# Scaling by g on the transposed tile, row products on the general-purpose engine, stores behind the transposes, and a third group of half products in one block

## The chip, the core and the metric

The kernel runs on one core of one Trainium2 chip. The core has five engines that run side by side and wait for each other by semaphores: TensorE (PE: matrix products; its weight loads are shown as PEld), VectorE (DVE), ScalarE (ACT), GpSimd (POOL) and SyncE (SP, which here issues DMAs). Sixteen DMA engines move data. The metric is the device time of one execution in microseconds (us), the median of several runs. The runs of one kernel lay within 0.1 to 0.6% of each other here. All runs used here were in the fast state.

## The reference

```python
kv  = einsum('bhsd,bhse->bhde', k, v)          # linear attention, 8 batches, 8 heads, 576 tokens, 64 wide
o   = einsum('bhsd,bhde->bhse', q, kv)
x   = o / sqrt(mean(o*o, -1) + 1e-6) * g_norm  # then as rows: x is [4608, 512]
g   = x @ w_gate;  val = x @ w_val             # 512 -> 1536
ffn = (gelu(g) * val) @ w_out                  # 1536 -> 512
out = x + sigmoid(x @ w_res) * ffn
```

The factor g_norm belongs to a column of x. In a row tile (tokens on partitions) it is a row vector of 512 values that is multiplied in element by element. In the transposed tile (columns on partitions) it is one scalar for each partition.

## The kernel before

The tokens are cut into nine blocks of 512: blocks 0 to 7 are the first 512 tokens of the eight batches, and the last block holds the remaining 64 of each. For each block there are groups of gate and value products (three groups of four columns of 128, "gps" and "vps" where they are direct), then the "outs": the residual gate and the product with w_out. The attention of a later block is fitted in between.

A group of 2x2 quarters may be done with seven products of half size instead of eight ("half products", Strassen's scheme). It needs sums of weights (wsg, wsv) and of tokens (ts), both made by DVE, and it has inner sums of its own: ACT copies A into E ("seed") and F into d ("keep"), DVE makes F = A + d and c = A + d, and PE then goes on in the same banks. Its order of work is a list of words; other work is hung onto words:

```python
"1g 1v Eg 5g Ev 5v dg 6g dv 6v Fg 2g Fv 2v 7g g11 7v cg 3g cv 3v h11 g12 4g g21 h12 4v g22 h21 h22"
# 1g..7v: products on PE; E, d: copies on ACT; F, c: sums on DVE; g..: gelu on ACT; h..: hid on DVE, h22 on POOL
```

In the kernel before, blocks 3 to 6 are "whole" (all three groups are half products) and block 2 has one direct group in front of two others. Blocks 7 and 8 have three such groups too, but the program does not count them as whole. Shortened, with names simplified and some lines joined:

```python
WHOLE = 3
GROUPS = {2: (1, 2), 3: (0, 1, 2), ..., 6: (0, 1, 2), 7: (1, 0, 2), 8: (0, 1, 2)}

def a_x(b, j, eng=nc.vector):            # g, on the rows, on DVE
    eng.tensor_tensor(out=t[:, j, :], in0=t[:, j, :], in1=g16, op=mult)
...
def first_two():                         # first half of a block's outs
    ...
    nc.scalar.copy(out=w["d"], in_=w["D"])
    aside("gates")
    for j in range(NJ):
        m_sigmoid(j)                     # ACT
...
def others():                            # second half
    prod(w["A"], s_[1], wo_t[:, 1], False);  aside("F")
    sub(nc.vector, w["F"], w["A"], w["d"], ADD);  aside("00")
    prod(w["E"], ...);  pf((0, 0), w["E"]);  aside("22")        # pf: gate product on DVE
    prod(w["A"], ...)
    c22 = res_all[...];  sub(nc.vector, c22, w["A"], w["d"], ADD);  aside("01")
    prod(w["F"], ...);  pf((0, 1), w["F"]);  aside("11")
    prod(w["A"], ...)                    # the last output product, in the bank that c22 was read from
    if whole(blk + 1):
        pf((1, 1), c22, nc.gpsimd);  pf((1, 0), w["A"])         # one gate product on POOL
    else:
        pf((1, 1), c22);  pf((1, 0), w["A"])
    for i in (1, 0):                     # + x on POOL, then the store
        fin((i, i));  fin((i, 1 - i));  store(i)
```

The transposes of x are DMAs issued by SP. In blocks 6 and later the residual gate is done in half products too, interleaved with the four sums hid_s of the hidden tile on DVE.

Of the kernel before, what the change touches and what calls it, by code (L numbers as in the profile page):

```python
# [18 lines left out]
def kernel(  # L19
# [307 lines left out]
    def where(b, j):  # L327
        return (b, j) if j < NJ else (B, pair(b))
# [22 lines left out]
        )  # L351

    def a_x(b, j, eng=nc.vector):
        blk, jj = where(b, j)
        eng.tensor_tensor(out=t_t[blk][:, jj, :], in0=t_t[blk][:, jj, :], in1=g16, op=ALU.mult)  # L355


    def d_qT(b):
# [222 lines left out]
    def res_in_halves(blk):  # L581
        return blk >= LAST[0] - 1

    def out_by_products(blk, later, banks, amid):
        w = {}
        s_ = hid_sums

        def aside(ahead_of):
            for f in amid.get(ahead_of, ()):
                f()  # L590

        def res(jj):
            for j in (2 * jj, 2 * jj + 1):
                m_res(blk, j, banks[j])

        def tiles_of_w():
            for n in ("D", "E", "F", "A"):
                w[n] = pmoe.tile([P, 2, CH], FP32, name="w" + n, bank=banks[n])
            w["d"] = attnp.tile([P, 2, CH], FP32, tag="sq", bufs=3, name="wd")

        def half(n, e, a, b):
            prod(w[n][:, e : e + 1], a, b, e == 0, (e,))

        def half_d(e):
            half("D", e, s_[0], wo_t[:, 0])

        def with_res():
            res_halves(blk, dict(zip("AFE", (banks[j] for j in range(3)))), {
                "sd": [tiles_of_w, lambda: half("A", 0, a_of(blk, 1, 1), b_of(1, 1)), lambda: s_sum(blk, 0)],
                "+F": [lambda: half("A", 1, a_of(blk, 1, 1), b_of(1, 1)), lambda: s_sum(blk, 1),  # L610
                       lambda: nc.scalar.copy(out=w["E"], in_=w["A"])],
                "+c": [lambda: s_sum(blk, 2), lambda: s_sum(blk, 3)],
                "tF": [lambda: half_d(0)],
            })
            half_d(1)
            nc.scalar.copy(out=w["d"], in_=w["D"])
            for j in range(NJ):
                m_sigmoid(j)

        def first_two():  # L620
            tiles_of_w()
            s_last(blk)
            prod(w["A"], a_of(blk, 1, 1), b_of(1, 1), True)
            nc.scalar.copy(out=w["E"], in_=w["A"])
            aside("D")
            prod(w["D"], s_[0], wo_t[:, 0], True)
# [3 lines that stand above are left out]
                m_sigmoid(j)  # L630

        def part(jj):
            return slice(None), slice(2 * jj[0], 2 * jj[0] + 2), slice(jj[1] * CH, (jj[1] + 1) * CH)

        def pf(jj, src, eng=nc.vector):
            eng.tensor_tensor(out=res_all[part(jj)], in0=th_all[part(jj)], in1=src, op=ALU.mult)  # L636

        def fin(jj):
            of = part(jj)
            nc.gpsimd.tensor_tensor(out=res_all[of], in0=res_all[of], in1=t_t[blk][of], op=ALU.add)  # L640

        def store(jj):
            dst = out[blk * S : blk * S + M0, :].rearrange("(p j) c -> p j c", j=NJ)
            js = slice(2 * jj, 2 * jj + 2)
            nc.sync.dma_start(out=dst[:, js, :], in_=res_all[:, js, :])

        def others():


            prod(w["A"], s_[1], wo_t[:, 1], False)  # L650
            aside("F")
            sub(nc.vector, w["F"], w["A"], w["d"], ALU.add)
            aside("00")
            prod(w["E"], a_of(blk, 1, 2), b_of(2, 1), False)
            pf((0, 0), w["E"])
            aside("22")
            prod(w["A"], s_[2], wo_t[:, 2], False)
            c22 = res_all[part((1, 1))]
            sub(nc.vector, c22, w["A"], w["d"], ALU.add)
            aside("01")  # L660
            prod(w["F"], s_[3], b_of(2, 2), False)
            pf((0, 1), w["F"])
            aside("11")
            prod(w["A"], a_of(blk, 2, 2), wo_t[:, 3], False)
            if whole(blk + 1):
                pf((1, 1), c22, nc.gpsimd)
                pf((1, 0), w["A"])
            else:
                pf((1, 1), c22)
                pf((1, 0), w["A"])  # L670
            if later:
                return
            for i in (1, 0):
                fin((i, i))
                fin((i, 1 - i))
                store(i)

        if later:
            x = [lambda j=j: a_x(blk, j) for j in range(NJ)]
            at_word(blk + 1, 0, "1v", *x[0:2])  # L680
            at_word(blk + 1, 0, "Fv", x[2])
            at_word(blk + 1, 0, "cv", x[3], lambda: fin((1, 0)), lambda: fin((1, 1)), lambda: store(1))
            at_word(blk + 1, 0, "h22", lambda: fin((0, 0)), lambda: fin((0, 1)), lambda: store(0))
        if res_in_halves(blk):
            return [with_res, lambda: None, lambda: None, others]
        return [lambda: res(0), lambda: res(1), first_two, others]
# [597 lines left out]
    def plan_attn_2():  # L1284
        b, m = 2, 1
        act = nc.scalar.copy
        at(m - 1, 2 * NF + 3, lambda: by_token(b, act, slice(0, 2)))
        at(m, 0, lambda: by_token(b, act, slice(2, 4)), lambda: attn_begin(b), lambda: d_qT(b))
        at(m, 2, lambda: a_kv(b))
        at(m, 3, lambda: load_behind(b))  # L1290
        at(m, 1, lambda: wo_sums(1))
        at(m, 3, lambda: wo_sums(3))
        at(m, 4, lambda: a_o(b))
        for j in range(NJ):
            at(m, 4 + j // 2, lambda j=j: a_ss(b, j))
        at(m, 6, lambda: a_norm(b, 0, NJ, nc.gpsimd))
        for j in range(NJ):
            at(m, 9 + j // 2, lambda j=j: a_t(b, j))
            at(m, 10 + j // 2, lambda j=j: a_x(b, j))
        at(m, 11, lambda: d_xT(b, 0, NJ))  # L1300

    WHOLE = 3
    GROUPS = {blk: (1, 2) for blk in range(2, WHOLE)} | {blk: (0, 1, 2) for blk in range(WHOLE, B - 1)} | {B - 1: (1, 0, 2), B: (0, 1, 2)}
    amid_gv = {}

    def at_word(blk, i, word, *fs):
        amid_gv.setdefault((blk, i), {}).setdefault(word, []).extend(fs)
# [5 lines left out]
    def plan_attn_ahead(b):  # L1313
# [22 lines left out]
        else:  # L1336
# [2 lines left out]
            at(m, NF - 1, lambda: a_kv(b, act))  # L1339
            at(m, NF, lambda: load_behind(b))  # L1340
        if rem:
            own = 2 * pair(b) + 1 == b
            at_word(m, last, "5v" if own else "3v", lambda: a_rem_kv(b))
            at_word(m, last, "dv" if own else "g12", lambda: kv_out(b))
            at_word(m, last, "h21", *[lambda: rem_mm(b)] * own, lambda: rem_out(b), lambda: a_sq(b, NJ))
# [6 lines left out]
        else:  # L1352
            at(m, NF + 3, *first)
        if whole(m + 1):
            t = [lambda j=j: a_t(b, j) for j in range(NJ + 1)]
            x = [lambda j=j: a_x(b, j) for j in range(NJ + 1)]
            for i, word, fs in (
                (0, "1v", t[2:3]),
                (0, "Fv", t[3:4]),
                (1, "1v", x[0:1]),  # L1360
                (1, "Fv", t[4:5]),
                (1, "cv", x[1:2]),
                (2, "1v", [*x[2:4], lambda: d_xT(b, 0, NJ)]),
                (2, "Fv", [x[4], lambda: d_xT(b, NJ, NJ + 1)]),
            ):
                at_word(m + 1, i, word, *fs)
            return
        for j in range(2, NJ + rem):
            at(m + 1, j - 2, lambda j=j: a_t(b, j))
        for j in range(NJ):  # L1370
            at(m + 1, 2 + j // 2, lambda j=j: a_x(b, j))
        at(m + 1, 3, lambda: d_xT(b, 0, NJ))
        if rem:
            at_word(m + 1, 0, "h21", lambda: a_x(b, NJ), lambda: d_xT(b, NJ, NJ + 1))

    units = [(n, g) for g in (1, 2, 0) for n in "gv"]
    sums = {u: weight_sums(u, nc.vector) for u in units}
# [10 lines left out]
    for blk in GROUPS:  # L1388
        t = token_sums(blk, nc.vector)
        if blk == 2:  # L1390
            at(blk - 1, NF + 3, *t)
            continue
        for key, f in zip(("00", "00", "22", "01") if whole(blk) else ("00", "22", "01", "11"), t):
            aside_out(blk - 1, key, f)
    wr_ = wr_sums(nc.vector)
    aside_out(LAST[0] - 2, "D", wr_[0])
    aside_out(LAST[0] - 2, "F", wr_[1])
    for word, f in (("Fv", wr_[2]), ("cv", wr_[3])):
        at_word(LAST[0] - 1, 2, word, f)
    out_at = {}  # L1400

# [39 lines left out]
    for blk in range(B + 1):  # L1441
# [21 lines left out]
        else:  # L1463
# [33 lines left out]
            def products(blk=blk, outs=outs):  # L1497
# [2 lines left out]
                if blk not in GROUPS:  # L1500
                    out_at[blk] = banks_behind()
                if blk < B:
                    outs.extend(out_by_products(blk, blk == 1, out_at[blk], amid_out.get(blk, {})))
                else:
                    outs.extend(out_last(blk, out_at[blk]))

# [53 lines left out]
```

## Time and profile before

| | before |
|---|---|
| median time | 323.15 us in the runs known beforehand, 322.93 us with one more |
| span of the profiled run | 320.7 us |
| PE, DVE, ACT, POOL busy | 312.7, 270.4, 203.9, 145.0 us |
| period of a whole block (start of its outs: 115.14, 148.01, 180.87 us) | 32.87 us |
| PE waits between the blocks | 0.22 us in all |

The last row is worked out from the TensorE timeline: the distance between the starts of two neighbouring groups of matmuls, less the regular 0.216 us for each 512-wide and 0.109 us for each 256-wide matmul, added up where it is over 0.12 us (from 25 us on). It is used in all the comparisons below, since PE's busy time cannot show short gaps. A timeline line gives the start in us, the duration in us, engine, line of the program, operation, output and inputs, shape, count, and in brackets the idle time before and what ended it.

Names in these lines: t is a row tile of x and xT its transpose, ts are sums of tokens, th is the sigmoid of the residual gate, osb the output, ge is gelu(g), hid the hidden tile gelu(g) * val, hid_s its sums, and wrs are sums of w_res. A, E, F, d and c are those of the half products, with w in front for the product with w_out and r for the residual gate; c22 is one quarter of the output, and op is the attention output. A bank is one of the buffers that PE writes products to. The program lets a product start in a bank only when what stood there has been read.

### The profile page before, as it was taken

The page shows a single profiled execution, that of the slowest core. Times are in us where ns is not written, and L with a number is a line of the kernel's source. Part 1 is how long each engine was busy: PE and PEld are TensorE (multiplying, and loading weights), DVE is VectorE, ACT ScalarE, POOL GpSimd, SP SyncE. Part 2 cuts the span into 40 slices and gives each one's busy share as a digit, 9 for nine tenths or more (in the row PEclk, how much of TensorE's full clock was granted, in tenths as well). Part 3 has the DMA queues.
Part 4 walks back from the last instruction along what each step waited for, and adds up shares of the span by engine and source line. Part 5 has one row for each costly group of instructions (what it writes and reads, how often), then busy time and mean ns, then how long its engine had stood idle before and what let it go on. Part 6 is the DMA issues. An engine that isn't in the chain of part 4 may idle for free.

```text
span 320.7 us, 7559 instructions
## 1 busy us (share of the span) xinstructions
PE 312.7 (97%) x2972; PEld 239.8 (75%) x2972; DVE 270.4 (84%) x492; ACT 203.9 (64%) x373; POOL 145.0 (45%) x212
## 2 busy tenths in 40 slices
PE   8899999999999999999999999999999999999993
PEld 3555754445858878887888688868888888888882
DVE  5888879799799888998899889999999677867774
ACT  3773685365727784878487848684767467736760
POOL 2792341573710979347843785117611242042232
PEclk9999999999999999999999999999999999999998
DMA  8999999799995599399938893620312030002004
GB/s 251 328 205 204 194 205 187 168 187 128 160 137 96 184 137 99 130 165 122 110 133 159 109 130 132 116 54 2 131 37 47 2 131 4 2 22 110 0 2 131
DMA packets 76693, 38.89 MB, mean 121 GB/s; under 512 B 42098, under 2 KB 74354, under 8 KB 76658
## 3 DMA queue, kind: packets, MB, share of 16 engines
q0 software_dynamic: 38752, 17.17, 42.5%
q1 hardware_dynamic: 37328, 20.71, 25.1%
q10 hardware_dynamic: 578, 0.52, 0.5%
q8 instruction: 23, 0.38, 0.5%
q14 instruction: 12, 0.10, 0.1%
HBM read 38.80 MB, written 9.44 MB: 150 GB/s over the span
## 4 chain that ended last, share of the span: by engine, by line
PE 92%; DVE 3%; DMA 2%; SPq 1%; issue 1%; POOL 0%; ACT 0%; DVEq 0%; ACTq 0%
PE Ag L871 11%; PE Av L871 11%; PE wA L500 11%; PE rps L415 7%; PE gps L395 6%; PE vps L395 6%; PE Fv L871 6%; PE Fg L871 6%; PE fps L432 3%; PE Eg L871 3%; PE Ev L871 3%; PE wF L500 3%; PE wE L500 3%; PE wD L500 3%; PE w L500 2%; PE kvp L208 2%
## 5 line engine op out<-in xcount | busy, mean ns | idle before, releaser
L908 POOL TENSOR_TENSOR hid<-ge,c 128x512 f16<-128x512 f16 x21 | 24.5, 1166 | 64.3 <-ACT ge L902 44.3
L640 POOL TENSOR_TENSOR osb<-osb,t 128x512 f32<-128x512 f32 x28 | 31.6, 1158 | 38.7 <-DVE osb L636 24.3
L500 PEld LDWEIGHTS <-hid_s 128*128 128x128 f16 x384 | 37.6, 98 | 4.3
L871 PEld LDWEIGHTS <-wsv 128*128 128x128 f16 x336 | 32.8, 98 | 4.1
L871 PEld LDWEIGHTS <-wsg 128*128 128x128 f16 x336 | 32.8, 98 | 3.8
L500 PEld LDWEIGHTS <-hid 128*128 128x128 f16 x288 | 28.2, 98 | 4.4
L881 ACT COPY Eg<-Ag 128x512 f32<-128x512 f32 x21 | 12.2, 583 | 25.9 <-PE Ag L871 25.9
L383 ACT ACTIVATE ge<-gps 128x512 f16<-128x512 f32 x24 | 14.1, 597 | 21.3 <-PE gps L395 21.1
L871 PEld LDWEIGHTS <-wv 128*128 128x128 f16 x252 | 24.6, 98 | 3.2
L871 PEld LDWEIGHTS <-wg 128*128 128x128 f16 x252 | 24.4, 98 | 3.3
L892 DVE TENSOR_TENSOR Fg<-Ag,d 128x512 f32<-128x512 f32 x21 | 14.7, 698 | 13.4 <-ACT d L885 9.0
L871 PE MATMUL Ag<-ts,wsg 128*128 128x256 f16 x168 | 25.2, 273 | 0.0
L871 PE MATMUL Av<-ts,wsv 128*128 128x256 f16 x168 | 25.2, 272 | 0.0
L254 DVE TENSOR_REDUCE ss<-sq 128x8 f32<-128x512 f32 x32 | 20.1, 678 | 5.4 <-ACT sq L249 5.4
L395 PE MATMUL gps<-xT,wg 128*128 128x512 f16 x88 | 22.6, 379 | 0.0
L415 PE MATMUL rps<-wr,xT 128*128 128x512 f16 x96 | 22.6, 380 | 0.0
L395 PE MATMUL vps<-xT,wv 128*128 128x512 f16 x88 | 22.6, 379 | 0.0
L500 PE MATMUL wA<-wo_ts,hid_s 128*128 128x256 f16 x168 | 20.6, 273 | 0.0
L384 DVE TENSOR_TENSOR hid<-ge,vps 128x512 f16<-128x512 f16 x24 | 16.3, 685 | 4.6 <-PE vps L395 3.8
L902 ACT ACTIVATE ge<-Eg 128x512 f16<-128x512 f32 x21 | 12.5, 597 | 10.3 <-PE Eg L871 10.3
L355 DVE TENSOR_TENSOR t<-t,g 128x512 f16<-128x512 f16 x36 | 18.9, 554 | 0.0
L341 DVE TENSOR_TENSOR t<-op,ny 128x512 f16<-128x512 f32 x28 | 18.3, 684 | 0.1
(210 smaller groups left out, 797.6 us busy)
## 6 DMA issues: line engine op xcount, KB each, us to landing
out_dram<-osb SPq DMA_DIRECT2D x14, 512.0 KB, 2.7
qraw<-in_q_dram POOLq DMA_DIRECT2D x7, 512.0 KB, 7.2
k<-in_k_dram POOLq DMA_DIRECT2D x7, 512.0 KB, 10.4
v<-in_v_dram POOLq DMA_DIRECT2D x7, 512.0 KB, 11.3
wg<-in_moe_w_gate_dram POOLq DMA_DIRECT2D x2, 512.0 KB, 8.4
wv<-in_moe_w_val_dram POOLq DMA_DIRECT2D x2, 512.0 KB, 9.0
wo<-in_moe_w_out_dram POOLq DMA_DIRECT2D x2, 512.0 KB, 14.0
out_dram<-osb SPq DMA_DIRECT2D x4, 256.0 KB, 4.8
```

The lines of the kernel that those rows point to most:

```text
L254: nc.vector.tensor_reduce(out=out_, in_=sqs.pop((b, i)), op=ALU.add, axis=mybir.AxisListType.X)
L341: nc.vector.tensor_tensor(out=t, in0=o, in1=scale, op=ALU.mult)
L355: eng.tensor_tensor(out=t_t[blk][:, jj, :], in0=t_t[blk][:, jj, :], in1=g16, op=ALU.mult)
L383: nc.scalar.activation(out=ge, in_=gps, func=AF.Gelu)
L384: nc.vector.tensor_tensor(out=hids[blk][:, f, :], in0=ge, in1=vps, op=ALU.mult)
L395: nc.tensor.matmul(ps[:, j0 * P : j1 * P], lhsT=w[:, cc, :], rhs=xT_t[blk][:, j0:j1, cc, :], start=(cc == 0 and j0 == 0), stop=(cc == NP - ...
L415: nc.tensor.matmul(rps, lhsT=xT_t[blk][:, j, cc, :], rhs=wr16[:, cc, :], start=(cc == 0), stop=(cc == NP - 1),)
L500: nc.tensor.matmul(ps[:, e - es[0], :], lhsT=a[:, f, e * P : (e + 1) * P], rhs=b[:, f, :], start=(start and e == es[0] and f == 0), stop=( ...
L640: nc.gpsimd.tensor_tensor(out=res_all[of], in0=res_all[of], in1=t_t[blk][of], op=ALU.add)
L871: nc.tensor.matmul(out_[:, r, :], lhsT=lhsT, rhs=rhs, start=(first and r == 0 and c == 0), stop=(c == 1), skip_group_check=True,)
L892: nc.vector.tensor_tensor(out=dst, in0=ps["A", u], in1=sb["d", u], op=ALU.add)
L908: eng.tensor_tensor(out=dst, in0=ge[q], in1=source(q, "v"), op=ALU.mult)
```

## The change

PE was busy all the time, so the intent was to take work from it: block 2's group 0 becomes a group of half products too. To make room on DVE for the sums that this needs, g is no longer multiplied into rows there. The tile is transposed without g and scaled afterwards in place, one scalar per partition; the rows, which are only needed for the final addition, get their g on POOL. The stores go behind the next block's transposes.

```diff
-    WHOLE = 3
+    WHOLE = 2
...
+    def a_g(b, j0, j1, eng=nc.vector):
+        xs = xT_t[blk][:, k0 : k0 + j1 - j0, :, :]
+        if eng is nc.scalar:
+            nc.scalar.activation(out=xs, in_=xs, func=AF.Copy, scale=gcol)
+        else:
+            eng.tensor_scalar(out=xs, in0=xs, scalar1=gcol, scalar2=None, op0=ALU.mult)
...
             if whole(blk + 1):
                 pf((1, 1), c22, nc.gpsimd)
                 pf((1, 0), w["A"])
+                aside("end")
             ...
+            if blk + 1 == WHOLE:
+                nc.gpsimd.tensor_copy(out=hold, in_=x_sums[blk + 1][0:1, 3, 1, 1, 0:1])
+            for j in range(NJ):
+                row_times_g(blk, j, nc.gpsimd)
...
+                at_word(blk + 1, 0, "h22", lambda i=i: fin((i, i)), lambda i=i: fin((i, 1 - i)))
+                at_word(blk + 1, 1, "h22", lambda i=i: store(i))
...
-        at(m, 11, lambda: d_xT(b, 0, NJ))                       # block 2's transpose
+        at(m, 10, lambda: d_xT(b, 0, NJ))
+        for i in range(2):
+            aside_out(m, "gates", lambda i=i: a_g(b, 2 * i, 2 * i + 2, nc.scalar))
...
         if blk == 2:
-            at(blk - 1, NF + 3, *t)
+            aside_out(blk - 1, "01", *t[0:2])
+            aside_out(blk - 1, "end", *t[2:4])
...
+    for p in range(B // 2):
+        at_word(LAST[0], 1 + p // 2, "h22", lambda p=p: row_times_g(B, p, nc.gpsimd))
-    for word, f in (("Fv", wr_[2]), ("cv", wr_[3])):
+    for word, f in (("1v", wr_[2]), ("h11", wr_[3])):           # sums of w_res, in block 6's group 2
```

Cut: the old placement of the row products, and the later blocks' transposes (now in group 0) and scalings (group 2).

More of the change, by code (lines that the diff above doesn't have):

```diff
@@ L353, in a_x, with row_times_g @@
     def a_x(b, j, eng=nc.vector):
-        blk, jj = where(b, j)
+        row_times_g(*where(b, j), eng)
+    def row_times_g(blk, jj, eng):
         eng.tensor_tensor(out=t_t[blk][:, jj, :], in0=t_t[blk][:, jj, :], in1=g16, op=ALU.mult)
+    def a_g(b, j0, j1, eng=nc.vector):
+        blk, k0 = where(b, j0)
+        xs = xT_t[blk][:, k0 : k0 + j1 - j0, :, :]
[3 more added lines that the diff above has]
+            eng.tensor_scalar(out=xs, in0=xs, scalar1=gcol, scalar2=None, op0=ALU.mult)
     def d_qT(b):
@@ L582, in res_in_halves, with out_by_products @@
         return blk >= LAST[0] - 1
-    def out_by_products(blk, later, banks, amid):
+    def out_by_products(blk, banks, amid):
         w = {}
@@ L670, in others, with rows_behind @@
                 pf((1, 0), w["A"])
-            if later:
-                return
-            for i in (1, 0):
-                fin((i, i))
-                fin((i, 1 - i))
-                store(i)
-        if later:
-            x = [lambda j=j: a_x(blk, j) for j in range(NJ)]
-            at_word(blk + 1, 0, "1v", *x[0:2])
-            at_word(blk + 1, 0, "Fv", x[2])
-            at_word(blk + 1, 0, "cv", x[3], lambda: fin((1, 0)), lambda: fin((1, 1)), lambda: store(1))
-            at_word(blk + 1, 0, "h22", lambda: fin((0, 0)), lambda: fin((0, 1)), lambda: store(0))
+            if blk + 1 == WHOLE:
+                nc.gpsimd.tensor_copy(out=hold, in_=x_sums[blk + 1][0:1, 3, 1, 1, 0:1])
+            for j in range(NJ):
+                row_times_g(blk, j, nc.gpsimd)
+            rows_behind()
+        def rows_behind():
+            for i in (1, 0):
+                at_word(blk + 1, 0, "h22", lambda i=i: fin((i, i)), lambda i=i: fin((i, 1 - i)))
+                at_word(blk + 1, 1, "h22", lambda i=i: store(i))
         if res_in_halves(blk):
@@ L1298, in plan_attn_2 @@
             at(m, 9 + j // 2, lambda j=j: a_t(b, j))
-            at(m, 10 + j // 2, lambda j=j: a_x(b, j))
-        at(m, 11, lambda: d_xT(b, 0, NJ))
-    WHOLE = 3
+        at(m, 10, lambda: d_xT(b, 0, NJ))
+        for i in range(2):
+            aside_out(m, "gates", lambda i=i: a_g(b, 2 * i, 2 * i + 2, nc.scalar))
+    WHOLE = 2
     GROUPS = {blk: (1, 2) for blk in range(2, WHOLE)} | {blk: (0, 1, 2) for blk in range(WHOLE, B - 1)} | {B - 1: (1, 0, 2), B: (0, 1, 2)}
@@ L1341, in plan_attn_ahead @@
         if rem:
+            at_word(m + 2, 0, "cv", lambda: a_g(b, NJ, NJ + 1))
             own = 2 * pair(b) + 1 == b
@@ L1354, in plan_attn_ahead @@
         if whole(m + 1):
-            t = [lambda j=j: a_t(b, j) for j in range(NJ + 1)]
-            x = [lambda j=j: a_x(b, j) for j in range(NJ + 1)]
+            t = [lambda j=j: a_t(b, j) for j in range(NJ)]
+            if rem:
+                at_word(m + 1, 0, "h21", lambda: a_t(b, NJ), lambda: d_xT(b, NJ, NJ + 1))
             for i, word, fs in (
                 (0, "1v", t[2:3]),
-                (0, "Fv", t[3:4]),
-                (1, "1v", x[0:1]),
-                (1, "Fv", t[4:5]),
-                (1, "cv", x[1:2]),
-                (2, "1v", [*x[2:4], lambda: d_xT(b, 0, NJ)]),
-                (2, "Fv", [x[4], lambda: d_xT(b, NJ, NJ + 1)]),
+                (0, "Fv", [t[3], lambda: d_xT(b, 0, NJ)]),
+                (2, "Fv", [lambda: a_g(b, 0, 2)]),
+                (2, "cv", [lambda: a_g(b, 2, NJ)]),
             ):
@@ L1369, in plan_attn_ahead @@
             at(m + 1, j - 2, lambda j=j: a_t(b, j))
-        for j in range(NJ):
-            at(m + 1, 2 + j // 2, lambda j=j: a_x(b, j))
-        at(m + 1, 3, lambda: d_xT(b, 0, NJ))
-        if rem:
-            at_word(m + 1, 0, "h21", lambda: a_x(b, NJ), lambda: d_xT(b, NJ, NJ + 1))
+        at(m + 1, 1, lambda: d_xT(b, 0, NJ))
+        at_word(m + 1, 1, "Fv", lambda: a_g(b, 0, 2))
+        at_word(m + 1, 1, "cv", lambda: a_g(b, 2, NJ))
     units = [(n, g) for g in (1, 2, 0) for n in "gv"]
@@ L1502, in products @@
                 if blk < B:
-                    outs.extend(out_by_products(blk, blk == 1, out_at[blk], amid_out.get(blk, {})))
+                    outs.extend(out_by_products(blk, out_at[blk], amid_out.get(blk, {})))
                 else:
```

## The prediction

> **What bounds the kernel now.** I read the page's busy table and slices first, then the chain that ended last, then the timeline of TensorE, and last the timelines of the other engines around the start of block 2, the only block whose matrix products change.
>
> ```profile
> PE 312.7 (97%) x2972; PEld 239.8 (75%) x2972; DVE 270.4 (84%) x492; ACT 203.9 (64%) x373; POOL 145.0 (45%) x212
> ...
> PE   8899999999999999999999999999999999999993
> ```
> ```profile
> PE 92%; DVE 3%; DMA 2%; SPq 1%; issue 1%; POOL 0%; ACT 0%; DVEq 0%; ACTq 0%
> ```
> PE is busy from end to end, and 92% of the chain that sets the end is PE work; DVE at 84% is second. Busy PE could still hide gaps, since ends of matmuls are modelled, so I looked at starts:
>
> ```profile
> 95.95 1.03 PE L395 MATMUL gps<-xT,wg 128*128 128x512 f16 x4
> 96.82 1.03 PE L395 MATMUL vps<-xT,wv 128*128 128x512 f16 x4
> 97.68 0.60 PE L871 MATMUL Ag<-xT,wg 128*128 128x256 f16 x4
> 98.12 0.60 PE L871 MATMUL Av<-xT,wv 128*128 128x256 f16 x4
> ```
> Four direct 512-wide matmuls recur every 0.864 us (96.82 to 97.68), four 256-wide ones every 0.437 us. Check for stalls: in the chain in order of time, the kv products of blocks 3, 4 and 5 begin at 109.44, 142.31 and 175.17, so a whole block takes 32.87 us. Its parts are 42 half products x 0.437 = 18.34, kv 0.75, residual gate 3.67, attention output 0.57, seven output products x 1.311 = 9.18, and about 0.25 for the remainder rows: 32.76. PE hardly waits anywhere between 20 and 314 us. Only PE work removed, or a new PE wait, can move the time.
>
> **What the Trainium skill says.** (1) "VectorE: DVE Perf Modes", the perf-mode tier table: fp16 tensor_tensor in SBUF reaches 2x, and 1x with an operand in PSUM; fp16 tensor_scalar and copy in SBUF reach 4x. The trace agrees: the 128x2048 f16 copy took 687 ns, rows times g at best 409 ns for 512 elements, and PSUM forms 680 to 700 ns. (2) "GPSIMD Engine Reference", Specifications: its SBUF interface is shared with VectorE and contends with VectorE instructions in a 2-port mode or with two SBUF inputs. The trace agrees:
>
> ```profile
> 131.40 1.16 POOL L908 TENSOR_TENSOR hid<-ge,c 128x512 f16<-128x512 f16 x1 [1.79 <-ACT ge L902]
> ```
> ```profile
> 131.70 1.14 DVE L355 TENSOR_TENSOR t<-t,g 128x512 f16<-128x512 f16 x1
> ```
> A DVE row product that starts inside a POOL instruction lasts 1.14 us instead of 0.41. The group runs from 409 to 1140 ns, mean 554. (3) "DMA: Bandwidth & Descriptors", Issuing engines are not separate DMA queues: transfers from all issuers interleave on the same 16 engines. The trace agrees: the transpose of block 2's tile, issued at 79.08 beside the load issued at 78.91, landed after 10.1 us against a median of 4.4.
>
> **The change, part by part.**
> *PE.* Block 2's group 0 was direct: 4 columns x 2 (gate, value) x 0.864 = 6.91 us. Now it is 7 products x 2 x 0.437 = 6.12 us. That is 0.80 us less, or 0.25%. No other PE instruction is added or removed.
> *DVE.* Of 36 row products, those of block 0 (4) stay; 32 x 0.554 = 17.7 us leave. In come g on the transposed tile: two of 128x1024 for each of blocks 3 to 7 and one of 128x512 for each of four rows of the last block. From the 687 ns copy, less 1024/4/0.96 = 267 ns, I estimate 0.42 us for 1024 elements and 0.29 for 512: 10 x 0.42 + 4 x 0.29 = 5.4 us. DVE falls by about 12 us plus one gate product (0.68) that goes to POOL. All of it lies beside PE.
> *ACT.* Two scalings of block 2's tile, 1.04 us each (the 128x1024 f16 copy on ACT), ahead of block 1's four sigmoids.
> *POOL.* 32 row products at about 1.16 us = 37 us, and one gate product at 1.27: 145 becomes about 183 us. In a whole block, counted from its start: the old block's gate product ends at 0.7, four row products at 5.4, hid of group 0 was ready at 7.1, four additions end at 12.9, and hid of group 1 was ready at 13.2. It fits, so I expect no PE wait from POOL there. Stores go out about 13 us into the next block, and their tile is written again some 16 us later; at 2.7 us to landing they cost nothing.
> *Transposes* are issued in group 0 and used in group 2, some 12 us later, against a landing of 4.4 us. Hidden, except for block 2.
>
> **The start of block 2** is where the 0.80 us can be lost. Before, 6.9 us of direct work stood ahead of the first half product there. Now the third product (after 0.87 us) needs token sums, and the other waits of a group come early as well.
>
> ```profile
> 84.61 0.60 ACT L627 COPY wd<-wD 128x512 f32<-128x512 f32 x1
> 85.07 2.22 ACT L429 ACTIVATE th<-th 128x512 f32<-128x512 f32 x4
> ```
> ```profile
> 87.10 0.69 DVE L636 TENSOR_TENSOR osb<-th,wE 128x512 f32<-128x512 f32 x1
> ...
> 90.97 0.69 DVE L636 TENSOR_TENSOR osb<-th,wA 128x512 f32<-128x512 f32 x1
> ```
> The transpose is issued about 77.2 (behind the two t at 75.83, without two row products). It queues behind qT's (landed near 78.3) and has some 2 us before the loads' data begin near 80.3; in before about 3.9 us of work took 8.8 us beside them. So 2.0 us of work at that share takes 4.4: landing near 85. ACT then scales from 85.1, and the first two sigmoids end near 88.1 instead of 86.2. From there, in steps of DVE (0.60 for a PSUM form, 0.34 to 0.45 for a sum): gate product to 88.7, weight sums 89.3, c22 89.9, two token sums 90.7, gate product 91.3, two t 92.5, gate product 93.1. That last one frees the bank of Ev 2.2 us into block 2 (which nominally starts at 90.94); in a whole block it is 1.4 us. Ev is copied by ACT (0.56, to 93.7), then two copies d (94.1, 94.6), then the two sums F on DVE (94.8, 95.4), and product 7 for value, nominally started at 94.87, starts at 95.4. That is 0.57 us of PE wait. POOL's new gate product becomes ready in the same instant as the two token sums; if it takes the shared interface between them, DVE is 1.1 us later and PE waits about 1.6 us. I weigh the two cases evenly: 0.57 to 1.6, mean 1.1.
>
> **End of block 7.** Two row products of the last block follow hid of group 2 on POOL (about 273.0 to 275.3) beside DVE's two-input hid_s sums at 273.46 and later, which took 0.95. Each may wait up to 0.7 us, and the sum in front of the last residual product is within 0.2 us of PE. I put 0.3 us (0 to 0.9) here. The small waits at 238 to 241 us (about 0.2 us, some behind row products) go away.
>
> **Sum.** -0.80 + 1.1 + 0.3 - 0.2 = +0.4 us by the full estimates. I trust the new waits less than the removed work, since slack that I can't see would swallow them, and take half of them: -0.80 + 0.7 - 0.1 = -0.2. So 323.15 becomes 323.0.
>
> **Rivals.** (a) The gain arrives whole: the transpose lands early, DVE's freed time absorbs the rest, and the time is 322.3. For it: DVE loses 12 us of work, and a whole block starts without waits. Against it: block 2's tile comes late, unlike those of later blocks. (b) The transpose lands as late as before (at 89 us). ACT, in order, holds the sigmoids, then the gate products, then the banks: about 4 us more at the start of block 2, giving 326. For it: 10.1 us before. Against it: it starts 1.9 us earlier, ahead of the loads. (c) POOL becomes the bound through its late additions and hid: 5 whole blocks x 1 us gives 327. Against it: 183 us of work in 320, and about 1.7 us free before each hid in the count above. (d) DVE was the bound, and 12 us less there gives several per cent. Against it: PE starts are gapless, so nothing is there to win.
>
> **Range and chances.** The sure term is -0.8; the uncertain ones run from 0 to about +3, and repeats spread over 0.6 us. So 321.8 to 325.2. Faster by 2% (316.7) would need PE idle time that isn't there: 0.01. Slower by 2% (329.6) needs (b) and (c) together: 0.02.
>
> **What would show it.** PE instructions for block 2: 168 matmuls of 128x256 in three groups, none of 128x512 for its gate and value. Right if TensorE's starts show one gap of 0.5 to 1.6 us within the first 5 us of block 2, Fg or Fv or the copy Ev being what it waits for, and later blocks still repeat every 32.87 us. The landing of block 2's transpose should be near 85 us and ACT's first sigmoid of block 1 about 2 us later than before. Wrong if block 2 starts gapless, if ACT stands idle for over 1 us in front of its scaling, if whole blocks grow longer than 32.9 us with POOL named in the waits, or if DVE doesn't lose some 12 us.

## The result, and the profile after

The changed kernel took 326.31 us (325.68 to 327.36, 4 runs) against 322.93 us (322.50 to 323.32, 4 runs). The ratio is 1.0108, with a 95% interval of 1.0077 to 1.0140. Ratios here are the mean time of one kernel's fast runs over that of the other's of the same rounds, so they are not quite the ratio of the medians. The kernel became 1.1% slower, 3.4 us, and the time lies above the stated range.

The busy table and the slices of PE on the page of the changed kernel:

```profile
PE 313.2 (97%) x2996; PEld 242.2 (75%) x2996; DVE 268.9 (83%) x476; ACT 208.2 (64%) x379; POOL 189.7 (59%) x247
...
PE   8999999999989999999999999999998999999993
```

The share of PE is the same 97% as before. Only two 8s in the row of 9s, in slices 12 and 31 of 40 (89 to 97 us and 243 to 251 us), hint at where it stood. The timeline of PE through the first of the two:

```profile
88.27 1.47 PE L511 MATMUL wF<-wo,hid_s 128*128 128x256 f16 x12
90.22 1.47 PE L511 MATMUL wA<-wo_ts,hid 128*128 128x256 f16 x12 [0.47 <-DVE osb L474]
91.52 0.60 PE L882 MATMUL Ag<-xT,wg 128*128 128x256 f16 x4
91.96 0.60 PE L882 MATMUL Av<-xT,wv 128*128 128x256 f16 x4
93.16 0.60 PE L882 MATMUL Fg<-ts,wsg 128*128 128x256 f16 x4 [0.60 <-DVE t L341]
93.75 0.60 PE L882 MATMUL Fv<-ts,wsv 128*128 128x256 f16 x4
94.19 0.60 PE L882 MATMUL Ag<-ts,wsg 128*128 128x256 f16 x4
95.01 0.60 PE L882 MATMUL Av<-ts,wsv 128*128 128x256 f16 x4 [0.22 <-ACT Ev L892]
```

Block 1's last output product, then block 2's first half products. The regular distance of the first line to the second is 1.31 us; it is 1.95. Between Av and Fg it is 1.20 instead of 0.44, between Ag and the next Av 0.82. With 0.15 us in front of Fv, the waits around the start of block 2 add up to 1.93 us. What PE waited for came late on DVE and ACT. ACT's and then DVE's timeline of the same stretch:

```profile
85.19 2.21 ACT L364 ACTIVATE xT<-xT,gcol 128x1024 f16<-128x1024 f16 x2
87.28 2.20 ACT L440 ACTIVATE th<-th 128x512 f32<-128x512 f32 x4
```
```profile
88.47 0.69 DVE L647 TENSOR_TENSOR osb<-th,wE 128x512 f32<-128x512 f32 x1 [1.40 <-ACT th L440]
...
89.48 0.68 DVE L474 TENSOR_TENSOR osb<-wA,wd 128x512 f32<-128x512 f32 x1
90.08 0.41 DVE L474 TENSOR_TENSOR ts<-xT 128x512 f16<-128x512 f16 x1
90.53 1.38 DVE L474 TENSOR_TENSOR ts<-xT,ts 128x512 f16<-128x512 f16 x1
...
92.43 1.27 DVE L341 TENSOR_TENSOR t<-op,ny 128x512 f16<-128x512 f32 x2
93.62 0.67 DVE L647 TENSOR_TENSOR osb<-th,wA 128x512 f32<-128x512 f32 x1
```
```profile
90.30 1.33 POOL L647 TENSOR_TENSOR osb<-th,osb 128x512 f32<-128x512 f32 x1 [0.63 <-DVE osb L474]
```

The two scalings push the sigmoids back by 2.1 us, DVE stands idle for 1.40 us for the first of them, and all its later work moves along: c22 (at 89.48; the last output product waits for it), the t whose banks Fg and Fv need (92.43), and the gate product that frees the bank of Ev (93.62; 90.97 before). On top, the second token sum takes 1.38 instead of 0.42 us: POOL's gate product began at 90.30, while the first sum was running, and ran beside the second until 91.63.

The second place is the end of block 6. The kernel before, POOL and then DVE:

```profile
241.17 1.21 POOL L908 TENSOR_TENSOR hid<-ge,c 128x512 f16<-128x512 f16 x1 [3.83 <-ACT ge L902]
254.55 4.50 POOL L640 TENSOR_TENSOR osb<-osb,t 128x512 f32<-128x512 f32 x4 [12.18 <-DVE osb L636]
```
```profile
243.07 0.95 DVE L463 TENSOR_TENSOR hid_s<-hid 128x1536 f16<-128x1536 f16 x1
243.96 0.70 DVE L575 TENSOR_TENSOR rF<-rA,rd 128x512 f32<-128x512 f32 x1
244.57 0.95 DVE L463 TENSOR_TENSOR hid_s<-hid_s,hid 128x1536 f16<-128x1536 f16 x1
```

and the changed kernel, POOL, DVE and PE:

```profile
242.01 1.27 POOL L919 TENSOR_TENSOR hid<-ge,c 128x512 f16<-128x512 f16 x1 [3.45 <-ACT ge L913]
243.25 6.09 POOL L357 TENSOR_TENSOR t<-t,g 128x512 f16<-128x512 f16 x4
```
```profile
242.78 0.79 DVE L474 TENSOR_TENSOR wrs<-wr,wrs 128x512 f16<-128x512 f16 x1
...
244.69 1.81 DVE L474 TENSOR_TENSOR hid_s<-hid 128x1536 f16<-128x1536 f16 x1
246.42 0.69 DVE L586 TENSOR_TENSOR rF<-rA,rd 128x512 f32<-128x512 f32 x1
247.02 1.30 DVE L474 TENSOR_TENSOR hid_s<-hid_s,hid 128x1536 f16<-128x1536 f16 x1
```
```profile
244.88 0.60 PE L559 MATMUL rA<-wrs,ts 128*128 128x256 f16 x4 [0.62 <-ACT rE L579]
...
247.16 0.60 PE L559 MATMUL rA<-wrs,ts 128*128 128x256 f16 x4 [0.60 <-DVE rF L586]
```

POOL, idle for 12.18 us here before, now runs block 6's four row products straight behind its hid. DVE's sums hid_s read two inputs from SBUF, as do POOL's products, and they take 1.81 and 1.30 us instead of 0.95. The sum rF behind them comes late, and PE waits. Another 0.78 us is lost a little earlier, where PE waits for a copy of ACT (rE) which itself waited for a hid on DVE. The waits in this place are 1.83 us against 0.22 before. At the end of block 7 the same happens with 0.50 us: there POOL runs row products from 275.60 us on, beside the sums.

The sum: 1.93 + 1.83 + 0.50 = 4.26 us of waits (without one of 0.13 us at 42 us, where the kernel before has 0.12) against 0.22, less 0.80 us of PE work, makes 3.24 us. The spans differ by 323.9 - 320.7 = 3.2 us. The whole blocks between are not slower: their outs begin at 116.53, 149.32 and 182.11 us, a period of 32.79 us against 32.87.

### The profile page after: what moved, and what is told of

It is laid out like the page before. It is cut to its first block, busy times and chain, and to the rows that moved or that the text cites. A ratio compares the mean times of both kernels' runs of the same rounds, so it can differ in the third digit from the quotient of the medians.

```text
span 323.9 us, 7633 instructions
## 1 busy us (share of the span) xinstructions
PE 313.2 (97%) x2996; PEld 242.2 (75%) x2996; DVE 268.9 (83%) x476; ACT 208.2 (64%) x379; POOL 189.7 (59%) x247
## 5 line engine op out<-in xcount | busy, mean ns | idle before, releaser
L919 POOL TENSOR_TENSOR hid<-ge,c 128x512 f16<-128x512 f16 x22 | 26.1, 1185 | 57.8 <-ACT ge L913 57.4
L357 POOL TENSOR_TENSOR t<-t,g 128x512 f16<-128x512 f16 x32 | 40.6, 1300 | 0.0
L882 PEld LDWEIGHTS <-wsg 128*128 128x128 f16 x352 | 34.4, 98 | 4.8 <-issue 0.8
L882 PEld LDWEIGHTS <-wsv 128*128 128x128 f16 x352 | 34.4, 98 | 4.7 <-issue 0.6
L651 POOL TENSOR_TENSOR osb<-osb,t 128x512 f32<-128x512 f32 x28 | 33.3, 1221 | 0.0
L394 ACT ACTIVATE ge<-gps 128x512 f16<-128x512 f32 x20 | 11.7, 597 | 14.3 <-PE gps L406 14.0
L903 DVE TENSOR_TENSOR c<-Ag,d 128x512 f32<-128x512 f32 x22 | 15.2, 689 | 4.4 <-PE Ag L882 4.4
L913 ACT ACTIVATE ge<-c 128x512 f16<-128x512 f32 x22 | 13.7, 625 | 7.7 <-DVE c L903 7.7
L406 PE MATMUL gps<-xT,wg 128*128 128x512 f16 x72 | 18.5, 379 | 0.0
L406 PE MATMUL vps<-xT,wv 128*128 128x512 f16 x72 | 18.5, 379 | 0.0
```

Of the source, the lines that this page charges most:

```text
L357: eng.tensor_tensor(out=t_t[blk][:, jj, :], in0=t_t[blk][:, jj, :], in1=g16, op=ALU.mult)
L394: nc.scalar.activation(out=ge, in_=gps, func=AF.Gelu)
L406: nc.tensor.matmul(ps[:, j0 * P : j1 * P], lhsT=w[:, cc, :], rhs=xT_t[blk][:, j0:j1, cc, :], start=(cc == 0 and j0 == 0), stop=(cc == NP - ...
L651: nc.gpsimd.tensor_tensor(out=res_all[of], in0=res_all[of], in1=t_t[blk][of], op=ALU.add)
L882: nc.tensor.matmul(out_[:, r, :], lhsT=lhsT, rhs=rhs, start=(first and r == 0 and c == 0), stop=(c == 1), skip_group_check=True,)
L903: nc.vector.tensor_tensor(out=dst, in0=ps["A", u], in1=sb["d", u], op=ALU.add)
```

## The experiments

Each kernel was correct. The first four ran on one chip in five rounds beside the kernel before (322.65 us), the last four likewise on another (322.62 us). The changed kernel was not run again beside them; its row is that of the result. The waits are those of the TensorE timeline, as defined above.

| kernel | median us | ratio to before (95%) | waits at block 2 | end of block 6 | end of block 7 |
|---|---|---|---|---|---|
| changed | 326.31 | 1.0108 (1.0077 to 1.0140) | 1.93 | 1.83 | 0.50 |
| rows of blocks 6, 7 held back | 324.58 | 1.0059 (1.0046 to 1.0072) | 1.92 | 0.77 | 0.52 |
| block 2 direct | 325.15 | 1.0075 (1.0061 to 1.0088) | 0.64 | 1.82 | 0.51 |
| two sigmoids first | 324.03 | 1.0046 (1.0028 to 1.0064) | 0 | 1.84 | 0.51 |
| the same, gate behind sums | 323.86 | 1.0032 (1.0020 to 1.0045) | 0 | 1.84 | 0.51 |
| hold and sigmoids | 322.74 | 1.0000 (0.9977 to 1.0023) | 0 | 0.77 | 0.51 |
| all repairs | 321.70 | 0.9961 (0.9940 to 0.9983) | 0 | 0.28 | 0 |
| all repairs, block 2 direct | 322.42 | 0.9985 (0.9965 to 1.0005) | 0 | 0.28 | 0 |
| scalings on VectorE | 324.81 | 1.0053 (1.0033 to 1.0073) | 0.49 | 1.83 | 0.50 |

**Rows of blocks 6 and 7 held back.** Is it POOL's row products that stretch DVE's sums?

```diff
-            if blk + 1 == WHOLE:
+            if blk + 1 == WHOLE or not whole(blk + 1):
                 nc.gpsimd.tensor_copy(out=hold, in_=x_sums[blk + 1][0:1, 3, 1, 1, 0:1])
```


> Edit: the row products of blocks 6 and 7 on POOL also wait for the next block's last token sum, as those of block 1 do. Theory A (in the changed kernel POOL has nothing in front of these rows, runs them right after the hid of group 2, and VectorE's two-input hid_s sums wait for the shared interface): the hid_s sums beside them return from 1.81 and 1.30 us to 0.95, PE's waits at the end of block 6 fall from 1.8 to about 0.8 us and at the end of block 7 from 0.5 to 0.3 us, so about 1.2 us less: ratio to before near 1.007 instead of 1.0108. Rival B (all of the loss is at the start of block 2): no change, 1.011. Rival C (POOL's added work as such is too much): no change or worse, since POOL only starts later.

Measured: ratio 1.0059. POOL and DVE at the end of block 6:

```profile
241.92 1.27 POOL L919 TENSOR_TENSOR hid<-ge,c 128x512 f16<-128x512 f16 x1 [3.44 <-ACT ge L913]
255.45 0.58 POOL L684 COPY hold<-ts 1x1 f16<-1x1 f16 x1 [12.26 <-DVE ts L474]
256.00 2.26 POOL L357 TENSOR_TENSOR t<-t,g 128x512 f16<-128x512 f16 x2
```
```profile
244.59 0.95 DVE L474 TENSOR_TENSOR hid_s<-hid 128x1536 f16<-128x1536 f16 x1
```

With the rows at 256 instead of 243 us the sum is back at 0.95 us, and the two waits behind it (0.76 and 0.29 us) are gone. So the rows of block 6 did cause them. It also rules out that block 2 is the only place, and that POOL has too much to do as such: here POOL does the same work later and the kernel is faster. The wait for ACT's rE (0.77 us) stayed, as expected, and block 7 kept its 0.5 us, where a fall to 0.3 had been expected: two rows of the last block, which the hold does not touch, still stood beside the sums there. The time fell by more than the 1.05 us of the waits (1.7 us in the medians); the changed kernel's four runs, from other rounds, spread over 1.7 us, and its profiled run was the fastest of them.

**Block 2 as before.** How much of the loss is the third group of half products?

```diff
-    WHOLE = 2
+    WHOLE = 3
```
(with the token sums of block 2 and the hold of block 1's rows kept where they were)

> Edit: block 2's group 0 as direct products again (block 2 not among the whole blocks), all else of the change kept. Theory A: PE gets 0.80 us of work back, but of the 1.9 us of waits around the start of block 2 only the one of the last output product (0.6 us, behind the delayed c22) stays: net 0.5 us less, ratio near 1.009; the waits at the end of blocks 6 and 7 (1.8 and 0.5 us) stay. Rival B (the third group in half products is the whole cause): ratio near 1.000. Rival D (the moves of g and of the stores cost everything, the third group gains its 0.8 us): ratio near 1.013.

Measured: ratio 1.0075. That is nearest to theory A's 1.009, but all three forecasts, 1.009 just as 1.000 and 1.013, lie outside the interval. It is the waits that speak for A: 0.64 us in front of the last output product stayed, the others around block 2 went, and blocks 6 and 7 kept theirs. So the third group is not the whole cause. Even without it the moves cost more than half of the loss.

**Two sigmoids first.** Is it ACT's order?

```diff
-            aside("gates")
             for j in range(NJ):
+                if j == 2:
+                    aside("gates")
                 m_sigmoid(j)
```


> Edit: in block 1, ACT does the first two sigmoids, then the two scalings of block 2's tile, then the other two. Theory A (ACT, in order, holds the first gate product and all of VectorE's work behind it by the 2.1 us of the scalings): first gate product from 88.5 back to about 87.2, the wait in front of the last output product (0.47 to 0.6 us) gone, PE's waits around the start of block 2 from 1.9 to about 0.6 us: 1.3 us less, ratio near 1.0068. Rival (the transpose lands late and ACT would wait for it wherever it stands): nothing gained, and the second pair of sigmoids later.

Measured: ratio 1.0046 (1.0068 had been expected), and no wait over 0.12 us at block 2 at all; 0.6 us had been expected to stay. DVE in this run:

```profile
87.15 0.69 DVE L648 TENSOR_TENSOR osb<-th,wE 128x512 f32<-128x512 f32 x1
...
89.46 0.42 DVE L474 TENSOR_TENSOR ts<-xT,ts 128x512 f16<-128x512 f16 x1
```

The first gate product is back at 87.15 us. The second token sum began at 89.46 and took 0.42 us: POOL was at work on the norm until 89.5 us, so its gate product no longer found the gap. The collision seen in the changed kernel was itself a result of the delay.

**The same, with POOL's gate product behind the second token sum.**

```diff
+                if blk + 1 == WHOLE:
+                    nc.gpsimd.tensor_copy(out=hold, in_=x_sums[blk + 1][0:1, 1, 1, 1, 0:1])
                 pf((1, 1), c22, nc.gpsimd)
```


> Edit: as the run before, and POOL's gate product at the end of block 1 waits for the second token sum. Theory A (that gate product takes the shared interface between the two token sums, which is why the second took 1.38 us and not 0.42): second sum back to 0.42, everything on VectorE behind it 0.95 us earlier, PE's waits at the start of block 2 down to 0.2 us or less: some 0.5 us less than the run before, ratio near 1.005, which is what the ends of blocks 6 and 7 alone cost less the 0.8 us. Rival (slack hides it): same as the run before.

Measured: ratio 1.0032; the interval overlaps that of the run before, whose waits it repeats to 0.01 us. The rival was right: there was no collision left to remove. The expectation rested on a collision that the edit before it had already taken away.

**Both repairs.** Do the two losses add? The edits are those of the runs with the rows held back and with two sigmoids first, together.

> Edit: both repairs at once, the row products of blocks 6 and 7 behind the next block's token sums, and the first two sigmoids ahead of the scalings. Theory A (the two losses are separate and add): the waits at block 2 (1.9 us) and the two behind hid_s sums in block 6 (1.05 us) both go, those behind wrs in block 6 (0.77) and in block 7 (0.5) stay: some 3.0 us less than the changed kernel, span near 320.9 us, ratio to before 1.000 to 1.002. Rival (they share a cause, so that the second repair gains little): ratio about 1.004.

Measured: ratio 1.0000, 322.74 us, span 320.8 us. They add, as expected.

**All repairs.** What is left of block 6 and block 7? On top of both repairs:

```diff
-    for word, f in (("1v", wr_[2]), ("h11", wr_[3])):
+    for word, f in (("1v", wr_[2]), ("Fv", wr_[3])):
-        at_word(LAST[0], 1 + p // 2, "h22", lambda p=p: row_times_g(B, p, nc.gpsimd))
+        at_word(LAST[p // 2], 1, "h22", lambda p=p: row_times_g(B, p, nc.gpsimd))
```


> Edit: as the run before, with the fourth sum of the residual gate's weights moved from behind the hid 11 of block 6's group 2 to the second-column word Fv of that group (ahead of POOL's hid there), and two of the last block's rows moved from the end of block 7 to block 8. Theory A: the remaining waits in block 6 (0.77 to about 0.2 us) and in block 7 (0.5 to 0) go, span near 319.9 us, ratio near 0.997: the 0.80 us of removed PE work arrives at last. Rival (the wait of rE in block 6 comes from the two scalings on VectorE, not from the weight sum): 0.5 us of it stays, ratio near 0.9985.

Measured: 321.70 us, ratio 0.9961: faster than both kernels. Its page begins

```profile
span 319.8 us, 7636 instructions
## 1 busy us (share of the span) xinstructions
PE 311.9 (98%) x2996; PEld 242.3 (76%) x2996; DVE 263.6 (82%) x476; ACT 207.9 (65%) x379; POOL 186.3 (58%) x249
```

and the span is 0.9 us below that of the kernel before, near the 0.80 us of removed work. The wait for rE fell from 0.77 to 0.28 us (0.22 before the change). In DVE's timeline of this run:

```profile
238.00 0.42 DVE L474 TENSOR_TENSOR wrs<-wr,wrs 128x512 f16<-128x512 f16 x1
```

So the place of the fourth weight sum was the cause of most of that wait: behind hid 11 it met POOL's hid and took 0.79 us, between two hid that PE was about to need; on the earlier word it took 0.42. The two scalings on DVE, which stayed, were not. Without the last block's two rows at its end, block 7 has no wait.

**All repairs, block 2 direct.** What does the third group bring when nothing else costs? On top of all repairs:

```diff
-    WHOLE = 2
+    WHOLE = 3
+                aside("end")
-            if blk + 1 == WHOLE or not whole(blk + 1):
+            if blk + 1 == 2 or not whole(blk + 1):
```
(the last two keep block 2's token sums and the hold of block 1's rows where they were)

> Edit: all repairs of the run before, but block 2's group 0 as direct products. Theory A: PE has 0.80 us more work and no other wait, so the span is 0.8 us longer than in the run before (near 320.7 us), ratio 0.999 to 1.001. Rival (the third group in half products brings waits of its own even when repaired): same time or shorter than the run before.

Measured: 322.42 us, 0.72 us more than the run before; the ratios differ by 0.0024, which is 0.77 us. The intervals overlap, but the five and five runs do not: the slowest with the third group (321.86) is below the fastest without it (322.33). That is the 0.80 us of the prediction. The ratio of 0.9985 (0.9965 to 1.0005) also shows that all the moves together, without the third group, gain nothing that is clear of the noise: 0.2 us in the medians, 0.5 by the ratio. PE had only 0.22 us of waits that DVE's freed time could have removed.

**Scalings on VectorE.** The same question as for the sigmoids, asked the other way round.

```diff
-            aside_out(m, "gates", lambda i=i: a_g(b, 2 * i, 2 * i + 2, nc.scalar))
+            aside_out(m, "gates", lambda i=i: a_g(b, 2 * i, 2 * i + 2))
```


> Edit: the changed kernel with block 2's two scalings on VectorE instead of ACT, nothing else. Theory A (it is ACT's order that costs, not the scaling or its transpose): sigmoids back to about 85.2 us, first gate product about 87.8 us behind two scalings of 0.48 us on VectorE; the second token sum still meets POOL's gate product, so part of the wait stays: PE waits at the start of block 2 from 1.9 to about 0.7 us, ratio near 1.007. Rival (the tile's late transpose is what all waits for): VectorE stands in front of its first scaling for over 1 us and the waits at block 2 stay near 1.9 us, ratio 1.010.

Measured: ratio 1.0053. DVE did not stand in front of its first scaling (two in 0.87 us from 86.15 us), the first gate product started at 87.94 us, and the waits at block 2 fell from 1.93 to 0.49 us (0.7 had been expected). So the tile was there in time, and it is the place in ACT's order that cost. The second token sum did not meet POOL's gate product (0.42 us), because POOL's norm was later; most of the rest of the wait is the bank of Ev (0.33 us).

## Why the prediction was wrong, point by point

**What bounds the kernel** was right: PE sets the end, its removed work arrives if nothing else waits, and DVE's freed time brought no gain clear of the noise by itself.

**PE, -0.80 us**, was right: 0.72 us between the two repaired kernels.

**The work beside PE** was counted with errors that didn't decide. ACT rose by 4.3 us, not by 2.1: the four copies of a group of half products (seed and keep, 0.58 us each) were forgotten, and a scaling took 1.17 instead of 1.04 us. DVE was to fall by about 12 us and fell by 1.5, which the prediction itself had named as a sign of being wrong. Its new group adds seven operations of 0.68 us for four, and much of the rest is time spent waiting for the shared interface, which the profile books as busy: in the repaired kernel, with the same instructions, DVE is busy for 263.6 us instead of 268.9. POOL rose to 189.7 us instead of 183; a row product took 1.30 us on average, with a median of 1.16.

**The start of block 2.** The mechanism was right and each of its times was close: the transpose landed at 84.4 us (near 85 had been said), the first gate product ended at 89.2 (88.7), and POOL took the interface between the two token sums (the worse of the two cases). The size was not: 1.93 us where 0.57 to 1.6 was said. The prediction followed only the bank of Ev. It had c22 ending at 89.9 us and did not hold that against the last output product, due at 89.6 in the same bank (0.64 us), nor the end of the two t against Fg and Fv, which need their banks (0.76 and 0.15 us).

**The end of block 7** was put at 0.3 us and took 0.50.

**The end of block 6** is the step that failed: new waits there aren't in the prediction. POOL's work was counted "in a whole block", with the rows behind "the old block's gate product" at 0.7 us after the block's start, and the count was taken as good for all blocks. In blocks 6 and 7 POOL has no norm and no gate product in the outs, so nothing holds the rows back, and they start beside the hid_s sums some 13 us earlier. The first experiment shows what that cost: 1.06 of the 1.61 us by which the waits grew there. The other part came mostly from the weight sum, whose new place the prediction did not look at: moving it removed 0.49 us. The prediction had the same mechanism for two rows at the end of block 7, but did not ask it of block 6. The one item that it booked near there came true and was small: the waits at 238 to 241 us (0.06 and 0.11 us before) are gone.

**The sum.** The new waits were added to 1.1 + 0.3 us and then halved "since slack that I can't see would swallow them". They measured 4.0 us more than before. The halving was the wrong way round: what the prediction did not see was not slack but more waits. With the full estimates the prediction would have been 323.55 us, still too low by 2.8 us.

**The rivals.** (a) became true only once the kernel was repaired. (b) did not happen: neither ACT nor, in the last experiment, DVE waited for the transpose. (c) did not happen: whole blocks repeat every 32.79 us. (d) is ruled out by the repaired kernel with block 2 direct.

## What to carry to other kernels

When work moves to an engine with slack, ask not only how much it has but what holds each piece back: where an in-order engine has nothing in front of it, the work starts at once, beside whatever it can disturb. On the path of an engine that is full, check each bank and each result that it needs against its due time one by one, since the waits add up over all of them. If a small gain arrives with a loss, look for the gaps in the starts of the bound engine; here three of them told where the repairs had to go, and 0.3% in the medians (0.4% by the ratio) was there in the end.

## What the Trainium skill lacked or had wrong

- "GPSIMD Engine Reference", Specifications, names the contention on the shared SBUF interface. No page that I found says how such a wait shows in a profile: here it is booked as busy on both sides. A two-input VectorE instruction that met one POOL instruction took 1.38 instead of 0.42 us, and 1.81 instead of 0.95 us beside a row of them; 32 row products on POOL ran from 1.14 to 1.87 us each.
- "VectorE: DVE Perf Modes", the perf-mode tier table: a tensor_scalar with a scalar per partition took 0.48 us for 128x1024 fp16 in SBUF (the mean of ten), above the 0.42 us that the prediction had estimated from the plain copy. No page that I found gives the cost of the scalar operand on VectorE.
- "DMA: Bandwidth & Descriptors", Issuing engines are not separate DMA queues, says that transfers interleave. How much a transpose suffers is not there: here it landed after 4.4 us at the median, 7.1 us when issued 1.8 us ahead of a load, 10.1 us when issued beside it.
